# The first MLP of a gated-attention and mixer kernel: preparing the last three weights later in the instruction order

## The chip, the cores and the metric

One core of a Trainium2 chip runs the whole program. The metric is device time in microseconds (us) of one execution. The five engines each take their own instructions in program order: TensorE (PE, with its weight loads as PEld), VectorE (DVE), ScalarE (ACT), GpSimd (POOL) and SyncE (SP), which issues the transfers.

## The reference

A linear attention with decay (its output is x), then a mixer with an MLP (the "first MLP"), then a gated MLP. Cut to what is computed:

```python
for t in range(S):                       # batch 4, heads 8, S 768, D 48
    state = alpha[:, :, t, :, None] * state + np.einsum('bhd,bhe->bhde', k[:, :, t], v[:, :, t])
    y[:, :, t] = np.einsum('bhd,bhde->bhe', q[:, :, t], state)
...
h = x.transpose(0, 2, 1) @ U @ V
u = x + h.transpose(0, 2, 1)             # 768 x 384 for each of 4 batches
x2 = u + np.maximum(u @ w_ch1, 0.0) @ w_ch2      # first MLP: 384 -> 1536 -> 384
...
h = np.maximum(x2 @ w_in, 0.0)
u, v = h[..., :512], h[..., 512:]
v_s = np.einsum('ts,bsd->btd', w_spatial, normalised(v)) + b_spatial[None, :, None]
out = (u * v_s) @ w_out
```

## The kernel before, in words

**Products in three parts.** TensorE multiplies in a short format, so each factor is kept as a high and a low part, and a product is three matmuls (L280 to L282, and L373 for the way up). A weight therefore has to be prepared before use.

**The twelve weights.** The hidden width 1536 of the first MLP is cut into 12 groups; "weight f" is the piece of both matrices for group f, one tile of 128 x 768 words. They arrive as 64-bit numbers. Class `Stage` prepares each in two stages, "begin" and "finish". `begin` issues, in this order, two DVE instructions that build a narrow word (L230 and L233, 128x768), one ACT instruction that scales the low words (L225) and one POOL addition (L240). `finish`, called the first time for a weight, issues an ACT copy, the high part (L586); called the second time, it issues a DVE subtraction, the low part (L245). In the traces and the instruction lists the tile of a prepared weight is `w`; the tenth, eleventh and twelfth weight are `w_1293`, `w_1465` and `w_1644`, and the twelfth is `w_1727` in the changed program.

**The order of the first batch.** The first batch's MLP runs weights 0 to 4 on both halves of the sequence side by side, then the halves in turn: weights 5 to 7, 8 and 9, 10 and 11. For each weight there is a way up (nine matmuls L373 into one of two "mm" banks: three with the high part of the weight and the high part of the input, three with the input's low part, three with the weight's low part), ACT's h (L380), DVE's hl (L361) and, two groups later, a way down (L280 to L282, and L433 when a half is done).

**What is woven in.** Between the matmuls the function `pull` is called. At the call numbers in the table `FIRST_STEPS` it runs `weights.finish` for "f" and `weights.begin` for "b"; from call 71 on it also runs, at an even pace, steps of the attention of the second batch (`attend`). The steps "f" and "b" of one call come ahead of an attention step of the same call. An attention pair (two heads, four pairs for a batch) goes through these steps: transposes (PE L757, ACT L760); the sums per chunk (PE L800, ACT L808), the scan over chunks (DVE L811, six instructions) that follows them, the states (ACT L821, L822); the scores (PE L773) and their masks (DVE L782, two instructions); the outputs (PE L832 with the masks, PE L842 with the states, ACT L857). The decays of the next pair are prepared in between (DVE scans L713 and L726, POOL L702, ACT L732 and L729). The mixer's product of a finished pair is PE L990; it writes the bank that L811 reads its decay factors from. Its low part is DVE L998.

The method that issues a finished weight is short; its two instructions are the two "f" of the table:

```python
def split(w, f=f):
    t = self.parts[f] = self.pool.tile([128, 2, 2 * E], F32R, name="w12", tag=f"f{f}")
    nc.scalar.activation(out=t[:, 0], in_=w, func=AF.Copy)      # L586
    yield
    rest(t[:, 1], w, t[:, 0], nc.vector)                        # L245
```

Of the kernel before, what the change touches and what calls it, by code (L numbers as in the profile page):

```python
# [68 lines left out]
N_WARM = 12  # L69
FIRST_STEPS = {  # L70
    5: "f", 6: "b", 13: "fbf", 22: "fbf", 31: "fbf", 34: "ss", 40: "fbf", 49: "fbf", 51: "ss", 58: "f", 59: "f",
    60: "b", 70: "ff", 80: "b", 89: "ff", 92: "b", 101: "fbf", 110: "ff",
}
AHEAD, N_AHEAD = 71, 4
BANKS = {"acc": 3, "mm": 2, "x": 3}
# [1466 lines left out]
```

## Time and profile before

| | before |
|---|---|
| median of 3 runs | 696.97 us (696.5 to 698.26) |
| profiled execution, its own time | 697.38 us |
| its span, first to last instruction | 695.7 us |
| busy share PE, DVE, ACT, POOL | 98%, 50%, 41%, 28% |
| mean granted clock of TensorE | 0.998 of full speed |

The profiled execution is 0.41 us above the median. A busy share is an average over the whole program; the stretch that the change touches lies between about 100 and 145 us of the span, and there the engines are loaded otherwise.

### The profile page before, as it was taken

To read this page: it belongs to the slowest core of one execution; us is meant where nothing else is said; L and a number is where in the kernel's file an instruction comes from. 1 tells how busy PE (TensorE), PEld (TensorE's weight loads), DVE (VectorE), ACT (ScalarE), POOL (GpSimd) and SP (SyncE) were. 2 spreads that over 40 slices of the span, in tenths; PEclk is the share of its full clock that TensorE was granted. 3 is DMA by queue.
4 is the path that set the end of the run, shared out by engine and by line. 5 is a ranking of instruction groups with operands and counts; after the bars stand their busy time and mean duration, and the time that the engine had idled before them with its cause. 6 is when DMAs were issued, how large, how long until landed. Compare 5 with 4: busy or idle time off the path is not lost.

```text
span 695.7 us, 14559 instructions
## 1 busy us (share of the span) xinstructions
PE 678.7 (98%) x6172; PEld 647.4 (93%) x6172; DVE 351.1 (50%) x651; ACT 283.8 (41%) x554; POOL 195.0 (28%) x165
## 2 busy tenths in 40 slices
PE   8999899999999999999999999999999999999996
PEld 7879898899999999999999999899899989999995
DVE  8989999766456335443333872541343152125211
ACT  3875467665454325554313553322232232123111
POOL 4434334341111131010210332351334223333211
PEclk9999999999999999999999999999999999999999
DMA  8699125333434304101006451401030003000001
GB/s 337 242 337 214 39 50 109 70 70 105 80 58 88 69 1 95 28 2 36 1 0 197 139 168 44 125 1 35 1 102 1 35 0 103 35 1 34 1 35 40
DMA packets 21210, 54.39 MB, mean 78 GB/s; under 512 B 2704, under 2 KB 12816, under 8 KB 19856
## 3 DMA queue, kind: packets, MB, share of 16 engines
q1 hardware_dynamic: 21136, 53.38, 28.3%
q8 instruction: 50, 0.82, 0.5%
q14 instruction: 24, 0.20, 0.1%
HBM read 42.75 MB, written 9.44 MB: 75 GB/s over the span
## 4 chain that ended last, share of the span: by engine, by line
PE 84%; DVE 8%; ACT 3%; DMA 2%; issue 1%; SPq 0%; POOL 0%; ACTq 0%; DVEq 0%
PE banks L373 20%; PE banks L280 18%; PE banks L281 18%; PE banks L282 18%; PE banks L842 2%; DVE bw L713 2%; DMA bits<-in_w 1%; DVE fw L726 1%; PE banks L800 1%; PE banks L832 1%; PE banks L773 1%; PE banks L757 1%; DVE narrow L230 1%; PE banks L974 1%; DVE after L811 1%
## 5 line engine op out<-in xcount | busy, mean ns | idle before, releaser
L373 PE MATMUL banks<-partuh,w 128*128 128x384 f32 x564 | 130.4, 338 | 2.3 <-DVE hl L361 2.3
L373 PEld LDWEIGHTS banks<-partuh,w 128*128 128x128 f32 x564 | 99.4, 188 | 3.7 <-DVE hl L361 2.9
L280 PE MATMUL banks<-h,w 128*128 128x384 f32 x288 | 98.2, 341 | 0.3
L361 DVE SCALAR_TENSOR_TENSOR hl<-banks,h 128x384 fp32r<-128x384 f32 x96 | 52.7, 550 | 86.7 <-ACT h L380 86.1
L281 PE MATMUL banks<-h,w 128*128 128x384 f32 x288 | 96.4, 335 | 0.0
L282 PE MATMUL banks<-hl,w 128*128 128x384 f32 x288 | 96.4, 335 | 0.0
L535 DVE TENSOR_TENSOR vsb<-banks,bb 128x384 f32<-128x384 f32 x32 | 17.9, 558 | 129.1 <-PE banks L282 129.1
L380 ACT ACTIVATE h<-banks 128x384 fp32r<-128x384 f32 x94 | 45.9, 488 | 83.7 <-PE banks L373 83.4
L541 ACT ACTIVATE gh<-gt 128x384 fp32r<-128x384 f32 x32 | 16.8, 525 | 126.2 <-DVE gt L538 126.2
L245 POOL TENSOR_TENSOR gl<-gt,gh 128x384 fp32r<-128x384 f32 x32 | 32.5, 1016 | 120.5 <-ACT gh L541 120.5
L281 PE MATMUL banks<-wsph,vl 128*128 128x384 f32 x192 | 65.1, 339 | 1.0 <-POOL vl L245 1.0
L373 PE MATMUL banks<-partul,w 128*128 128x384 f32 x282 | 66.0, 341 | 0.0
L280 PE MATMUL banks<-wsph,vh 128*128 128x384 f32 x192 | 64.9, 338 | 0.0
L282 PE MATMUL banks<-wspl,vh 128*128 128x384 f32 x192 | 64.8, 338 | 0.0
L245 POOL TENSOR_TENSOR partul<-ub,partuh 128x384 fp32r<-128x384 f32 x43 | 42.9, 1023 | 69.6 <-ACT partuh L316 56.8
L280 PEld LDWEIGHTS banks<-h,w 128*128 128x128 f32 x288 | 54.0, 188 | 1.6 <-issue 0.8
L281 PEld LDWEIGHTS banks<-h,w 128*128 128x128 f32 x288 | 54.1, 188 | 0.0
L282 PEld LDWEIGHTS banks<-hl,w 128*128 128x128 f32 x288 | 54.1, 188 | 0.0
L373 PEld LDWEIGHTS banks<-partul,w 128*128 128x128 f32 x282 | 49.2, 188 | 0.8
L702 POOL TENSOR_TENSOR akq<-akq,fw 128x768 f32<-128x768 f32 x14 | 25.1, 1795 | 77.4 <-DVE fw L726 65.3
L240 POOL TENSOR_TENSOR narrow<-narrow,bits 128x768 uint32<-128x768 uint32 (+1 forms) x14 | 28.4, 2033 | 54.1 <-ACT seen L729 20.5
L245 POOL TENSOR_TENSOR vl<-vt,vh 128x512 fp32r<-128x512 f32 x20 | 27.2, 1386 | 49.8 <-ACT vh L505 49.8
(204 smaller groups left out, 1373.0 us busy)
## 6 DMA issues: line engine op xcount, KB each, us to landing
akq<-in_akq SPq DMA_DIRECT2D x24, 434.4 KB, 7.4
bits<-in_w SPq DMA_DIRECT2D x12, 768.0 KB, 11.6
x2d<-ub SPq DMA_DIRECT2D x8, 576.0 KB, 3.8
ub<-x2d SPq DMA_DIRECT2D x8, 576.0 KB, 4.9
out_y<-ob SPq DMA_DIRECT2D x24, 192.0 KB, 1.9
v<-in_v SPq DMA_DIRECT2D x15, 288.0 KB, 7.6
words<-in_w_in SPq DMA_DIRECT2D x8, 384.0 KB, 3.3
words<-in_wsT SPq DMA_DIRECT2D x4, 576.0 KB, 5.5
```

The lines of the kernel that those rows point to most:

```text
L240: nc.gpsimd.tensor_tensor(out=t, in0=t, in1=low, op=ALU.add)
L245: engine.tensor_tensor(out=out, in0=x, in1=hi.bitcast(F32), op=ALU.subtract)
L280: nc.tensor.matmul(out=ps, lhsT=wh, rhs=xh, start=first, stop=False)
L281: nc.tensor.matmul(out=ps, lhsT=wl, rhs=xh, start=False, stop=False)
L282: nc.tensor.matmul(out=ps, lhsT=wh, rhs=xl, start=False, stop=last)
L361: nc.vector.scalar_tensor_tensor(out=hl, in0=ps[:, 0:TB], scalar=0.0, in1=h.bitcast(F32), op0=ALU.max, op1=ALU.subtract)
L373: nc.tensor.matmul(out=ps[:, 0:TB], lhsT=wx[:, k * 128 : (k + 1) * 128], rhs=ux[:, k, :], start=i == 0, stop=i == len(parts) - 1)
L380: nc.scalar.activation(out=h, in_=ps[:, 0:TB], func=AF.Relu)
L535: nc.vector.tensor_tensor(out=vsb, in0=psv[:, 0:TB], in1=self.g["bb"][:, blk * TB : (blk + 1) * TB], op=ALU.add)
L541: nc.scalar.activation(out=hi, in_=gt, func=AF.Copy)
L702: engine.tensor_tensor(out=chunks(x)[:, c], in0=chunks(x)[:, c], in1=chunks(by)[:, c, 1:CW], op=ALU.mult)
L713: nc.vector.tensor_tensor_scan(out=bw[:, ::-1], data0=a[:, 1 : AW + 1][:, ::-1], data1=ends[:, ::-1], initial=0.0, op0=ALU.mult, op1=ALU.max)
```

## The change

Three steps of the table are put at later call numbers, one at a time: the second "f" of call 89 goes to 93, the "bf" of call 101 goes to 107 (its "f" and "b" in the other order), and the two "f" of call 110 go to 116 and 119.

```diff
 FIRST_STEPS = {
     5: "f", 6: "b", 13: "fbf", 22: "fbf", 31: "fbf", 34: "ss", 40: "fbf", 49: "fbf", 51: "ss", 58: "f", 59: "f",
-    60: "b", 70: "ff", 80: "b", 89: "ff", 92: "b", 101: "fbf", 110: "ff",
+    60: "b", 70: "ff", 80: "b", 89: "f", 92: "b", 93: "f", 101: "f", 107: "fb", 116: "f", 119: "f",
 }
```

No instruction is added or taken away; the transfers' queue (SP) is unchanged. On DVE, at the second attention pair of the second batch, the rows read so (`-` before, `+` changed; `sm` are the masked scores, `narrow` and `bits` the words of a weight that is being begun, here the eleventh):

```order
 L811 SCALAR_TENSOR_TENSOR after<-add,banks 128x96 x6
+L782 TENSOR_TENSOR sm<-banks,causal 128x384 x2
+L230 TENSOR_SCALAR narrow<-bits 128x768
+L233 SCALAR_TENSOR_TENSOR narrow<-bits,narrow 128x768
 L245 TENSOR_TENSOR w_1293<-narrow,w_1293 128x768
-L782 TENSOR_TENSOR sm<-banks,causal 128x384 x2
-L230 TENSOR_SCALAR narrow<-bits 128x768
-L233 SCALAR_TENSOR_TENSOR narrow<-bits,narrow 128x768
 L726 SCALAR_TENSOR_TENSOR fw<-akq_86,starts 128x780
```

The low part of the tenth weight moves from in front of the masks to behind them and behind the begin of the eleventh weight.

On DVE at the third pair, behind the third copy of sums L433 of a finished half:

```order
 L433 TENSOR_TENSOR ub<-banks,ub 128x384 x3
-L230 TENSOR_SCALAR narrow<-bits 128x768
-L233 SCALAR_TENSOR_TENSOR narrow<-bits,narrow 128x768
+L811 SCALAR_TENSOR_TENSOR after<-add,banks 128x96 x6
+L782 TENSOR_TENSOR sm<-banks,causal 128x384 x2
+L361 SCALAR_TENSOR_TENSOR hl<-banks,h 128x384
+L726 SCALAR_TENSOR_TENSOR fw<-akq_84,starts 128x780
 L245 TENSOR_TENSOR w_1465<-narrow,w_1465 128x768
```

The low part of the eleventh weight (L245) moves from in front of the scan L811 to behind the masks and L726, and the begin of the twelfth (L230, L233), which stood ahead of it, comes behind it.

On ACT, from the third pair's outputs to the fourth pair's, the twelfth weight's scaling (L225) and its copy (L586) stand here:

```order
 L729 ACTIVATE seen<-bw 128x12
+L225 ACTIVATE bits<-bits 128x768
 L857 ACTIVATE ub<-banks 48x384 [waits DVE_49,PE_49]
...
 L380 ACTIVATE h<-banks 128x384 [waits PE_49]
-L586 ACTIVATE w_1644<-narrow 128x768 [waits Pool_49]
 L760 ACTIVATE kn<-banks 128x384 [waits DVE_49,PE_49]
...
 L732 ACTIVATE fw,over<-akq_84,below 128x780 [waits Pool_49]
 L380 ACTIVATE h<-banks 128x384 [waits PE_49]
+L586 ACTIVATE w_1727<-narrow 128x768 [waits Pool_49]
 L729 ACTIVATE seen<-bw 128x12
```

The copy L586 moves past the fourth pair's transposes, sums (L808), states (L821, L822), the L732 and the h of the next group. L225 stood before between the two copies L981 ahead of the third pair's L808.

On PE the order is the same; the first three matmuls of the twelfth weight's first way up stand in front of the mixer's product L990 and the fourth pair's outputs, with these waits:

```order
-L373 MATMUL banks<-partuh,w_1644 128x384 x3
+L373 MATMUL banks<-partuh,w_1727 128x384 [waits Activation_49]
+L373 MATMUL banks<-partuh,w_1727 128x384 x2
 L990 MATMUL banks<-yb,u_97 96x128 [waits DVE_49]
 L990 MATMUL banks<-yb,u_97 96x128 x5
 L832 MATMUL banks<-sm,v 48x64 [waits DVE_49] x2
 L832 MATMUL banks<-sm,v 48x64 x22
-L842 MATMUL banks<-akq_84,state 48x64 [waits Activation_49] x2
-L842 MATMUL banks<-akq_84,state 48x64 x20
+L842 MATMUL banks<-akq_84,state 48x64 x22
```

The wait on ACT that stood at L842 now stands at the first matmul with the twelfth weight.

## Rows read from the trace of the kernel before

**Rows 1.** Page, busy us, share of the span and instructions of each engine

```profile
PE 678.7 (98%) x6172; PEld 647.4 (93%) x6172; DVE 351.1 (50%) x651; ACT 283.8 (41%) x554; POOL 195.0 (28%) x165
```

**Rows 2.** Waits of PE, 84 to 150 us: total, times, longest

```profile
PE banks L990 <- DVE after L811: 1.5, 1, 1.5
PE banks L832 <- DVE sm L782: 0.7, 2, 0.5
```

**Rows 3.** Timeline of PE, second pair: start, duration, then the instruction, [idle before]

```profile
109.68 0.31 PE L832 MATMUL banks<-sm,v 64*48 64x64 f32 x2 [0.53 <-DVE sm L782]
110.14 0.90 PE L832 MATMUL banks<-sm,v 64*48 64x64 f32 x46 [0.15 <-DVE sm L782]
110.98 1.46 PE L842 MATMUL banks<-akq,state 128*48 128x64 f32 x44
```

**Rows 4.** Timeline of DVE, second pair

```profile
108.22 0.93 DVE L245 TENSOR_TENSOR w<-narrow,w 128x768 fp32r<-128x768 f32 x1
109.07 1.02 DVE L782 TENSOR_TENSOR sm<-banks,causal 128x384 f32<-128x384 f32 x2
```

**Rows 5.** Timeline of ACT, second pair

```profile
109.53 1.18 ACT L822 ACTIVATE state<-after 64x528 f32<-64x528 f32 x1
```

**Rows 6.** Timeline of DVE, third pair

```profile
118.87 1.60 DVE L230 TENSOR_SCALAR narrow<-bits 128x768 uint32<-128x768 uint32 x1
120.50 0.96 DVE L233 SCALAR_TENSOR_TENSOR narrow<-bits,narrow 128x768 uint32<-128x768 uint32 x1
121.38 0.95 DVE L245 TENSOR_TENSOR w<-narrow,w 128x768 fp32r<-128x768 f32 x1
122.25 1.57 DVE L811 TENSOR_TENSOR_SCAN after<-add,banks 128x96 f32<-128x96 f32 x6
...
127.62 0.56 DVE L361 SCALAR_TENSOR_TENSOR hl<-banks,h 128x384 fp32r<-128x384 f32 x1 [2.89 <-ACT h L380]
128.09 1.77 DVE L726 TENSOR_TENSOR_SCAN fw<-akq,starts 128x780 f32<-128x780 f32 x1
```

**Rows 7.** Timeline of PE, third pair

```profile
123.87 1.55 PE L990 MATMUL banks<-yb,u 128*96 128x128 f32 x12 [1.53 <-DVE after L811]
```

**Rows 8.** Timeline of ACT, third pair

```profile
117.55 0.96 ACT L225 ACTIVATE bits<-bits 128x768 uint32<-128x768 uint32 x1
...
119.10 0.67 ACT L808 ACTIVATE add<-banks 128x576 f32<-128x576 f32 x1
...
127.12 0.47 ACT L380 ACTIVATE h<-banks 128x384 fp32r<-128x384 f32 x1
...
130.35 0.84 ACT L586 ACTIVATE w<-narrow 128x768 fp32r<-128x768 f32 x1
```

**Rows 9.** Timeline of POOL, 118 to 132 us

```profile
118.34 1.72 POOL L702 TENSOR_TENSOR akq<-akq,bw 128x768 f32<-128x768 f32 x1
...
130.01 1.69 POOL L702 TENSOR_TENSOR akq<-akq,fw 128x768 f32<-128x768 f32 x1 [5.99 <-PE banks L373]
```

**Rows 10.** Timeline of DVE, 110 to 137 us, other rows

```profile
110.00 0.55 DVE L230 TENSOR_SCALAR narrow<-bits 128x768 uint32<-128x768 uint32 x1
...
133.02 1.48 DVE L433 TENSOR_TENSOR ub<-banks,ub 128x384 f32<-128x384 f32 x3
134.41 1.77 DVE L713 TENSOR_TENSOR_SCAN bw<-akq,ends 128x780 f32<-128x780 f32 x1
...
136.37 1.52 DVE L811 TENSOR_TENSOR_SCAN after<-add,banks 128x96 f32<-128x96 f32 x6
```

**Rows 11.** Timeline of PE, fourth pair: its sums' end, the twelfth weight's begin

```profile
134.09 0.23 PE L800 MATMUL banks<-ident,nothing 64*64 64x48 f32 x2
...
138.05 0.69 PE L373 MATMUL banks<-partuh,w 128*128 128x384 f32 x3
```

**Rows 12.** Timeline of PE, its last instruction

```profile
688.55 0.34 PE L282 MATMUL banks<-woutl,gh 128*128 128x384 f32 x1
```

**Rows 13.** Windows: stretch, length, busy PE, PEld, DVE, ACT, POOL, granted clock, DMA, GB/s

```profile
692.00:693.00 1.00, 0.00 (x0) 0.00 (x0) 0.00 (x0) 0.00 (x0) 0.00 (x0) 0.73 0.09 27
```

## The prediction

> **What bounds the kernel now.** The page says that TensorE is busy for 98% of the span [rows 1], so the time is PE's own work plus its few idle stretches, and an edit on another engine counts only as far as it moves one of these. The second view is PE's waits in the stretch that the table's late calls touch: two entries stand out there, the mixer's product L990 behind the scan L811 (1.5 us) and the outputs L832 behind the masks (0.7 us) [rows 2]. The third view is the timeline of each engine around the two places, to see what is queued ahead of the instruction that PE waits for. Last, since the change moves one weight's copy a long way down ACT's queue, the timeline at the place where PE first uses that weight. Times below are on the clock of the trace before.
>
> **First move: the masks of the second pair.** DVE does the tenth weight's low part at 108.22 and the masks only at 109.07, 0.85 us later [rows 4]; PE stands 0.53 + 0.15 us for them [rows 3]. With L245 behind the masks these are done 0.85 us earlier and L832 no longer waits. But the next matmuls, L842, need the states, and ACT's L822 ends at 109.53 + 1.18 = 110.71 [rows 5] whatever DVE does behind L811; L842 started at 110.98 [rows 3]. So of 0.68 us at most 110.98 - 110.71 = 0.27 us is gained; the rest becomes a wait on ACT. The bound below is zero. I take **0.25 us**. The moved L245 ends near 111.6 (108.2 + 1.02 for the masks, 0.55 + 0.96 for the begin that is now ahead of it, 0.93 of its own [rows 4, 6, 10]); PE is busy with L842 until 112.4 [rows 3] and reaches the tenth weight only behind it, so that costs nothing.
>
> **Second move: the scan of the third pair.** DVE runs L230, L233 and L245 from 118.87 to 122.25 in front of L811, 3.38 us [rows 6]; L811 then ends at 123.82 and L990 starts at 123.87 after 1.53 us of idle PE [rows 7]. L811's input is ready when ACT's L808 ends, 119.10 + 0.67 = 119.77, or up to 0.8 us earlier, since the L225 of 0.96 us ahead of it is gone too [rows 8]. So L811 starts between 119.0 and 119.8 (I take 119.0; DVE is free at 118.9) and ends by 121.4, before PE arrives at 122.3 - 0.25. The masks behind it (1.0 us) and the two states (2.4 us) end by 122.5 and by 123.8 at the latest, ahead of L832 at about 123.5 and L842 at about 124.3. The whole 1.53 us goes, with about 0.05 more, since a matmul behind a wait does not overlap the one before: **1.55 us**, between 1.2 and 1.6. PE is then 1.8 us ahead.
>
> **Third move: the twelfth weight.** Here a wait is added. PE meets this weight at 138.05 [rows 11], with the gains at 138.05 - 1.8 = 136.25. Before, ACT copied it (L586) at 130.35 [rows 8], long ahead. Now the copy stands behind L821, L822, L732 and L380 of the fourth pair, and L821 waits for that pair's L811. How long this takes is read from the third pair: from L811's start (122.25) to L380's start (127.12) 4.87 us, then 0.47 for L380 and 0.84 for L586 [rows 6, 8]: the weight is ready 6.2 us after the fourth pair's L811 starts. Queued behind the waiting matmul on PE are L990 and the outputs L832 and L842, all of which could have run; nothing else is late for them.
>
> When does that L811 start? From the third pair's (119.0), along DVE's new order, start to start:
> - to L361: 5.37 (122.25 to 127.62, ACT's chain) = 124.4; L361 0.47 and L726 1.77 [rows 6] = 126.6; L245 0.95 = 127.55.
> - L230. POOL's L702 becomes ready 1.92 us behind L726's start (128.09 to 130.01) [rows 6, 9], here at 126.8, while L245 runs. Alone L230 takes 0.55 us [rows 10]; at 118.87, begun during an L702 that ran from 118.34 to 120.06, it took 1.60 and ended 0.41 behind it [rows 6, 9]. If L702 runs as soon as L245 ends, to 129.2, L230 ends at 129.65; if L230 goes first, at 128.1.
> - L233 0.96; then L998 and L361, about 0.7 together; L433 to L713 1.39, L713 to L811 1.96 [rows 10]: 129.65 + 0.9 + 0.7 + 1.4 + 1.95 = **134.6**, less some 0.1 of overlaps, 134.5.
>
> In the other case DVE is ready 1.5 us earlier, and what L811 then waits for is its input, at 133.2 (the bound below). So PE gets its weight at 134.5 + 6.2 = 140.7, less 0.1 for the overlap of L380 and L586: 140.6. It stands from about 136.3 to 140.6, **4.3 us**, and the program is 140.6 - 138.05 = **2.5 us** behind before from there on.
>
> On L230 the Trainium skill (SBUF — State Buffer, "Who interferes with whom") says that the port pair that VectorE and GpSimd share is an exclusive lock: the one that starts first has it for its whole instruction and the other is blocked. The 1.60 us of L230 agree. By that rule the sum is 2.5; with shared bandwidth and no lock it would lie between 1.4 and 2.5.
>
> **The sum.** 4.3 - 1.8 = 2.5 us longer. Own time of the profiled execution 697.38 (span 695.7 and 1.68 around it), so 699.9 for it; it was 0.41 above the median of 696.97, and on the median the forecast is **699.5 us**. Bounds without another mechanism: the fourth pair's sums on PE end at 134.32 [rows 11], with the gain at 132.5; L808 (0.7) follows, so L811 starts at 133.2 at the earliest, and with 6.1 us behind it the weight cannot come before 139.3, 1.3 us late. At the other end L811 may start at 134.9 and the second move give only 1.2: 3 us. What remains of the program is bound by PE, so that nothing gives this back: the other engines only gain room. The twelfth weight's low part is used some 4 us behind its high part (L990, L832 and L842 stand between: 1.55 + 0.9 + 1.46 [rows 3, 7]) and DVE needs 0.95 for it: nothing.
>
> **The rivals.**
> - *A shorter wait.* L230 goes ahead of POOL, or DVE's rows overlap more; L811 starts at 133.2, the weight comes at 139.4, and the loss is 1.35 us: **698.3**. For it: DVE's next instruction is already in its queue. Against: in the trace POOL had the port whenever it came first, and here it has waited since 126.8.
> - *The clock falls in the wait.* PE's last matmul ends at 688.89 [rows 12]; in 692 to 693 the granted clock averages 0.73, a fall from full (2.4 GHz) to half (1.2 GHz) at 692.46, 3.6 us behind it [rows 13]. The mean of the whole span is 0.998 of full speed, so the wait of 1.53 us did not lower it noticeably. A wait of 4.3 us could, and the matmuls behind it would take twice as long until it rises. No row shows how long that lasts; from below nothing, and I take a low clock of 3.6 us, as long as the idle before the fall, a choice: 1.8 us more, **701.3**. The Trainium skill (TensorE: Matmul & The Clock Gate, "Why this matters for your kernels") warns of long idle gaps between bursts of matmuls, which speaks for this rival.
> - *The copy is in time.* Only the gains are left, 697.0 - 1.8 = **695.2**, faster. That needs L586 done by 136.25, so the fourth pair's L811 begun at 130.1, before PE has even made the sums that it scans (132.5). It would take a chain of 3.3 us instead of 6.2 from L811 to the copy and no DVE work ahead, so I hold it for nearly excluded.
>
> **How the numbers follow.** The forecast 0.58, with a range of its own of 698.8 to 700.2; the shorter wait 0.18; the fallen clock 0.20; the copy in time 0.04. A difference of 0.3%, 2.1 us, is about what a measurement of this kernel tells from none; the bound lies at 699.1, inside the forecast's own range, so some eight of ten of its chance count as slower (0.48), with the fallen clock's 0.20 in all 0.68. The rest of the forecast and the shorter wait make 0.28 for the same, and 0.04 remain for faster. The range of 698.1 to 701.4 takes in the three cases that are slower in some degree.
>
> **What the profile of the changed kernel would show.** Right: no idle of PE before the third pair's L990, at L832 of the second pair at most a trace, a short wait of L842 on L822; one idle stretch of 3.8 to 4.6 us before the L373 that stands ahead of the fourth pair's L990, put down to ACT's L586; that L586 directly behind an L380; the fourth pair's L811 at about 134.5; L230 of the twelfth weight at 1.6 us or more, ending with POOL's L702. Clock: 1.00 from 130 to 150, or a window under 1.00 near the end of the wait. Wrong it would be if the copy's wait is under 2 us, if L990 still waits for L811, or if a second wait of PE appears in the fourth pair's outputs or the mixer's sums behind.

## The result, and the profile after

The changed kernel takes 704.62 us (median of 5 runs, 702.6 to 706.71), the kernel before 697.28 (5 runs, 696.5 to 698.26): a ratio of 1.0105, 95% interval 1.0091 to 1.012, so 7.3 us slower where 2.5 were forecast. The profiled execution is the longest of the five: 706.71 us, with a span of 704.9 against 695.7. Its accounts below must come to 9.2 us, not to 7.3.

PE's waits from 84 to 180 us of the changed kernel (total, times, longest):

```profile
PE banks L373 <- ACT w L586: 3.0, 1, 3.0
PE banks L757 <- issue: 2.4, 1, 2.4
PE banks L832 <- issue: 0.5, 1, 0.5
PE banks L990 <- ACT yb L981: 0.3, 1, 0.3
```

Of [rows 2] the wait of L990 behind L811 is gone, as forecast, and the forecast wait for the twelfth weight's copy L586 is there, with 3.0 us for 4.3. A second wait of 2.4 us, at L757 (the fourth pair's transposes), was not forecast. Its releaser is given as "issue", so the view names no cause. PE's timeline has the places:

```profile
110.43 0.96 PE L832 MATMUL banks<-sm,v 64*48 64x64 f32 x37
111.94 0.42 PE L832 MATMUL banks<-sm,v 64*48 64x64 f32 x11 [0.55 <-issue]
112.29 1.45 PE L842 MATMUL banks<-akq,state 128*48 128x64 f32 x44
...
123.53 1.47 PE L990 MATMUL banks<-yb,u 128*96 128x128 f32 x12
...
132.45 0.85 PE L757 MATMUL banks<-ident,akq 128*128 128x128 f32 x6 [2.44 <-issue]
...
135.12 1.16 PE L373 MATMUL banks<-partuh,w 128*128 128x384 f32 x3
...
137.83 0.79 PE L373 MATMUL banks<-partul,w 128*128 128x384 f32 x3
...
144.79 1.33 PE L373 MATMUL banks<-partuh,w 128*128 128x384 f32 x3 [3.01 <-ACT w L586]
145.92 2.76 PE L990 MATMUL banks<-yb,u 128*96 128x128 f32 x12
```

Besides the two waits, look at the durations. L990 took 1.47 us at 123.53 and 2.76 at 145.92 for the same twelve matmuls, and three L373 took 1.16 and 1.33 where the undisturbed ones take 0.69 [rows 11]. Windows of one microsecond say why (stretch, length, busy PE, PEld, DVE, ACT, POOL, granted clock, DMA, GB/s):

```profile
84.00:85.00 1.00, 1.00 (x5) 1.00 (x4) 1.00 (x3) 0.00 (x0) 0.00 (x0) 0.50 0.00 0
135.00:136.00 1.00, 1.00 (x5) 0.98 (x4) 0.64 (x2) 0.00 (x0) 0.00 (x0) 0.50 0.02 8
137.00:138.00 1.00, 1.00 (x49) 0.95 (x50) 0.84 (x2) 0.73 (x3) 0.26 (x1) 0.91 0.00 0
144.00:145.00 1.00, 0.21 (x1) 0.21 (x2) 0.79 (x2) 0.85 (x3) 0.00 (x0) 0.51 0.00 0
...
150.00:151.00 1.00, 1.00 (x28) 0.93 (x22) 0.00 (x0) 0.00 (x0) 0.00 (x0) 0.58 0.06 16
```

The granted clock is at half (1.2 GHz) behind each wait: from 133.8 to 137.2 behind the wait at L757, and from 144.0 to 150.8, beginning within the wait for L586. A third stretch, 82.6 to 86.0, lies before the place of the change, behind a wait of 2.3 us (L373 behind L361) that the profile of before has too, there with the clock at 1.00.

On DVE and ACT the timeline shows what the two waits hang on. DVE first:

```profile
120.60 1.58 DVE L811 TENSOR_TENSOR_SCAN after<-add,banks 128x96 f32<-128x96 f32 x6 [0.31 <-ACT add L808]
...
128.16 0.93 DVE L245 TENSOR_TENSOR w<-narrow,w 128x768 fp32r<-128x768 f32 x1
129.01 2.04 DVE L230 TENSOR_SCALAR narrow<-bits 128x768 uint32<-128x768 uint32 x1
131.08 0.96 DVE L233 SCALAR_TENSOR_TENSOR narrow<-bits,narrow 128x768 uint32<-128x768 uint32 x1
132.07 0.28 DVE L998 TENSOR_TENSOR stk<-banks,stk 32x128 fp32r<-32x128 f32 x1
...
138.69 1.57 DVE L811 TENSOR_TENSOR_SCAN after<-add,banks 128x96 f32<-128x96 f32 x6 [0.82 <-ACT add L808]
```

Then ACT, and POOL:

```profile
137.97 0.69 ACT L808 ACTIVATE add<-banks 128x576 f32<-128x576 f32 x1 [0.24 <-PE banks L800]
...
143.91 0.83 ACT L586 ACTIVATE w<-narrow 128x768 fp32r<-128x768 f32 x1
...
128.38 2.24 POOL L702 TENSOR_TENSOR akq<-akq,fw 128x768 f32<-128x768 f32 x1 [7.03 <-DVE fw L726]
```

L998 takes the mixer's product of the third pair out of its bank, and it now stands behind L245, L230 and L233. It ends at 132.07 + 0.28 = 132.35, and L757 starts at 132.45. The code says that the two share a bank: the product's bank is `ps_g` in place `ALONE`, and `tags = {"flip": (ALONE, PAIR[0])}` gives that place to the transposes of the next pair. Before, L998 ended at 130.28 and L757 started at 130.38, the same 0.1 us behind it, and PE had no idle there. The rows of the kernel before, of DVE and of PE, which the account below uses too:

```profile
130.00 0.28 DVE L998 TENSOR_TENSOR stk<-banks,stk 32x128 fp32r<-32x128 f32 x1
```

```profile
106.43 0.93 PE L773 MATMUL banks<-akq 64*64 64x64 f32 x48
...
130.38 0.85 PE L757 MATMUL banks<-ident,akq 128*128 128x128 f32 x6
...
134.25 0.80 PE L373 MATMUL banks<-partul,w 128*128 128x384 f32 x3
```

**The account.** Differences of the same instruction's start, after minus before, along PE, in the two profiled executions: scores L773 of the second pair +1.35 (107.78 against 106.43: the low clock at 82.6 to 86.0); L842 +1.31; L990 of the third pair -0.34; L757 of the fourth +2.07; the L373 five microseconds behind it +3.58 (137.83 against 134.25); the twelfth weight's first L373 +6.74; the next L373 with that weight +9.61 (151.79 against 142.18); the span +9.2. So the first move brought 0.04, the second 1.65; the wait at L757 cost 2.4 and the low clock behind it 1.5; the wait for the copy cost 3.2 and the low clock behind it 2.9. The two waits less the two gains are 3.9 us and the low clock behind the waits is 4.4; the 1.35 us of the stretch at 82.6 lie ahead of the change, and 0.4 us are gone again by the end.

### The profile page after: what moved, and what is told of

Its sections match the earlier page's. It is cut to its first block, busy times and chain, and to the rows that moved or that the text cites. A ratio compares the mean times of both kernels' runs of the same rounds, so it can differ in the third digit from the quotient of the medians.

```text
span 704.9 us, 14559 instructions
## 1 busy us (share of the span) xinstructions
PE 685.3 (97%) x6172; PEld 653.4 (93%) x6172; DVE 351.8 (50%) x651; ACT 283.8 (40%) x554; POOL 194.7 (28%) x165
## 4 chain that ended last, share of the span: by engine, by line
PE 86%; DVE 5%; ACT 3%; DMA 2%; issue 1%; POOL 1%; SPq 1%; ACTq 0%; DVEq 0%; POOLq 0%
PE banks L373 20%; PE banks L280 18%; PE banks L281 18%; PE banks L282 18%; PE banks L842 2%; PE banks L800 1%; PE banks L832 1%; PE banks L773 1%; PE banks L757 1%; DVE fw L726 1%; DMA bits<-in_w 1%; DVE bw L713 1%; PE banks L974 1%; PE banks L393 1%; PE banks L990 1%
## 5 line engine op out<-in xcount | busy, mean ns | idle before, releaser
L373 PE MATMUL banks<-partuh,w 128*128 128x384 f32 x564 | 132.3, 343 | 5.3 <-ACT w L586 3.0
L373 PEld LDWEIGHTS banks<-partuh,w 128*128 128x128 f32 x564 | 100.7, 190 | 7.0 <-ACT w L586 3.3
L361 DVE SCALAR_TENSOR_TENSOR hl<-banks,h 128x384 fp32r<-128x384 f32 x96 | 52.6, 549 | 86.5 <-ACT h L380 85.9
L380 ACT ACTIVATE h<-banks 128x384 fp32r<-128x384 f32 x94 | 45.8, 488 | 85.4 <-PE banks L373 85.1
L373 PE MATMUL banks<-partul,w 128*128 128x384 f32 x282 | 66.5, 343 | 0.0
L245 POOL TENSOR_TENSOR gl<-gt,gh 128x384 fp32r<-128x384 f32 x32 | 32.4, 1014 | 120.6 <-ACT gh L541 120.6
L245 POOL TENSOR_TENSOR partul<-ub,partuh 128x384 fp32r<-128x384 f32 x43 | 42.8, 1022 | 75.7 <-ACT partuh L316 63.0
L373 PEld LDWEIGHTS banks<-partul,w 128*128 128x128 f32 x282 | 49.6, 189 | 0.8
L702 POOL TENSOR_TENSOR akq<-akq,fw 128x768 f32<-128x768 f32 x14 | 25.6, 1827 | 80.6 <-DVE fw L726 80.6
L245 POOL TENSOR_TENSOR vl<-vt,vh 128x512 fp32r<-128x512 f32 x20 | 27.1, 1381 | 49.8 <-ACT vh L505 49.8
```

What stands on the lines that cost most here:

```text
L245: engine.tensor_tensor(out=out, in0=x, in1=hi.bitcast(F32), op=ALU.subtract)
L361: nc.vector.scalar_tensor_tensor(out=hl, in0=ps[:, 0:TB], scalar=0.0, in1=h.bitcast(F32), op0=ALU.max, op1=ALU.subtract)
L373: nc.tensor.matmul(out=ps[:, 0:TB], lhsT=wx[:, k * 128 : (k + 1) * 128], rhs=ux[:, k, :], start=i == 0, stop=i == len(parts) - 1)
L380: nc.scalar.activation(out=h, in_=ps[:, 0:TB], func=AF.Relu)
L702: engine.tensor_tensor(out=chunks(x)[:, c], in0=chunks(x)[:, c], in1=chunks(by)[:, c, 1:CW], op=ALU.mult)
```

## The experiments

Each was compared with the kernel before on its own chip (medians 698.31 of 14 and 698.34 of 23 runs there), so the ratios are what to compare, not the times.

**The begin one call later.** Theory: L757 waits for L998, which stands behind the twelfth weight's begin. The rival was a wait for POOL's L702 or for the port that DVE and POOL share; a reason of PE's own, as the word "issue" would have it, would leave the wait as it is too. At call 108 the two steps come behind L998.

```diff
-... 101: "f", 107: "fb", 116: "f", 119: "f",
+... 101: "f", 108: "fb", 116: "f", 119: "f",
```

> The changed kernel with one step moved by one call, 107 to 108, so that the mixer's low part L998 stands on DVE ahead of L245, L230 and L233. Theory: the 2.44 us of idle PE before the fourth pair's L757 are a wait for L998, which reads the bank that L757 writes. Then that wait is gone (under 0.3 us), the wait for the twelfth weight's copy L586 grows from 3.0 to about 4.2 us, since PE comes to it earlier, and a clock fallen behind one wait costs about 3 us: 702.8 us, 701 to 704. Rival: L757 waits for POOL's L702 (the q of the same pair) or for the shared port. Then moving L998 alone does nothing, the wait stays at 2.0 to 2.8 us and the time near 704.6.

Measured: 703.67 us, ratio 1.0074 (1.0057 to 1.009). PE's waits, then DVE's timeline, then PE's:

```profile
PE banks L373 <- ACT w L586: 4.5, 1, 4.5
...
```

```profile
129.63 0.28 DVE L998 TENSOR_TENSOR stk<-banks,stk 32x128 fp32r<-32x128 f32 x1 [1.30 <-ACT stk L997]
129.95 1.04 DVE L245 TENSOR_TENSOR w<-narrow,w 128x768 fp32r<-128x768 f32 x1
```

```profile
130.02 0.85 PE L757 MATMUL banks<-ident,akq 128*128 128x128 f32 x6
...
142.31 1.33 PE L373 MATMUL banks<-partuh,w 128*128 128x384 f32 x3 [4.48 <-ACT w L586]
143.43 2.76 PE L990 MATMUL banks<-yb,u 128*96 128x128 f32 x12
```

With L998 ahead of L245 the wait at L757 is gone: it was L998. The rival, POOL's L702, is out, since here it ended at 130.18, behind the start of L757 at 130.02. The wait for the copy is now 4.5 us, close to the forecast's 4.3, since PE comes to it 2.4 us earlier. The clock fell in it, at 140.4, with PE idle since 137.8, and stayed at half to 147.2; L990 again took 2.76. From the first L373 to the next behind L842 it is 148.82 - 142.31 = 6.5 us, before 4.13 (142.18 - 138.05): 2.4 us for the clock.

**The copy at call 112.** The other wait by itself: the wait at L757 stays, and the copy L586 comes early enough.

```diff
-... 107: "fb", 116: "f", 119: "f",
+... 107: "fb", 112: "f", 119: "f",
```

> The changed kernel with the twelfth weight's copy L586 at call 112 in place of 116, so that ACT runs it between the two copies L981 of the third pair and ahead of the fourth pair's states. Theory: the wait of 3.0 us before the first matmul with the twelfth weight is gone, and with it the clock that fell behind it; the wait before L757 stays at 2.4 us, with a clock fall of up to 1.5 us behind it. Sum against before: 2.4 - 1.65 = 0.75 without and 2.3 with the fall: 698 to 699.6 us. Rival: the loss comes from the port shared by DVE and POOL and not from the copy's place; then at most 1 us is given back, 703.6 or more.

Measured: 699.6 us, ratio 1.0017 (1.0004 to 1.0031). PE's waits:

```profile
PE banks L757 <- issue: 2.4, 1, 2.4
...
```

The wait of 2.4 us stays, the one for L586 is gone, and the clock is at half from 133.4 to 136.8. Less the second move's 1.65 us, the wait makes 0.75 us and the clock about 1.5, 2.2 in all; 1.2 were measured (0.3 to 2.2). The ten executions suggest why it is less. Their mean granted clock is 0.993 in the profiled one and up to 0.998 in others, and the two with 0.998 have spans of 695.6 and 696.4, which is what the kernel before takes on that chip at a mean clock of 0.997 or 0.998 (694.9 to 695.7) plus about 0.75. So the wait of 2.4 us seems to have lowered the clock in some executions only; no trace of those is kept.

**Only the copy late.** The kernel before with the third move alone.

```diff
-... 101: "fbf", 110: "ff",
+... 101: "fbf", 116: "f", 119: "f",
```

> The kernel before with only the last two steps of the change: the two finishing steps of the twelfth weight at calls 116 and 119 in place of 110. Nothing is gained ahead. Theory: the fourth pair's L811 starts at 136.4 us of the span as before, the copy is ready 6.1 us later, and PE stands 4.3 us before its first matmul with the twelfth weight: 701.6 us without the clock, and about 704 (702.5 to 705) with a clock fallen at the end of that wait for some 5 us. No other wait of PE is added. Rival (the clock falls by chance wherever it falls, in before too): 701.6 us with the mean granted clock at 0.998.

Measured: 702.18 us, ratio 1.0055 (1.0032 to 1.0078). PE's waits:

```profile
PE banks L373 <- ACT w L586: 3.0, 1, 3.0
...
```

Then ACT's and DVE's timelines:

```profile
136.00 0.69 ACT L808 ACTIVATE add<-banks 128x576 f32<-128x576 f32 x1
```

```profile
136.72 1.58 DVE L811 TENSOR_TENSOR_SCAN after<-add,banks 128x96 f32<-128x96 f32 x6
```

The time lies below the expected 702.5 to 705, because the wait was 3.0, not 4.3: with the begin at its old place and the low part at 119, DVE was free when the fourth pair's sums came, and L811 started 0.72 us behind the start of L808. So 3.0 us is the wait with an undelayed L811. In the run at call 108 L811 started at 136.31, 1.6 us behind the end of L808, and DVE was busy up to it: the other 1.5 us of that run's wait stem from the eleventh weight's low part and the twelfth's begin, which stand in front of it there. The clock, 144.2 to 147.6 at half, makes the rest: 702.18 - 698.31 is 3.9 us. Here too one of the five executions has a mean clock of 0.998, and its span of 698.4 is that of the kernel before at such a clock plus the 3.0 us of the wait alone.

**Filling the waits with matmuls.** Is the low clock caused by the idle of PE? Matmuls whose results nobody uses were put in both waits of the changed kernel. If the idle is the cause, the waits remain in the time and the low clock goes.

```diff
+                if isinstance(b, int) and b == 0 and blk == 0 and f == NF1 - 1:
+                    busy(6, ps.banks[:, 3, :])
                 h = self.up_group(block, f)
...
+                if n == 2 * NP - 1:
+                    busy(5, ps.banks[:, 3, :])
                 pair.flip()
```

> The changed kernel with extra matmuls that need nothing and whose result is not used (identity by identity, about 0.44 us each at full clock): 5 ahead of the fourth pair's L757 and 6 ahead of the first matmul with the twelfth weight, so that PE has work in both waits. The waits themselves stay. Theory: the falls of the clock follow from the two idle stretches; with PE busy in them the granted clock stays at 1.00 from 125 to 155 us, and the time is before's plus 2.4 + 3.0 - 1.65 = 3.8, near 701 us (700.3 to 702.3). Rival: the falls come from elsewhere (the load of PE ahead, or the phase of the run); then the clock falls there as often and the time stays within 1 us of 704.6.

Measured: 704.69 us, ratio 1.0086 (1.0069 to 1.0103): a miss. PE's waits (the lines from the first insertion on have moved by two; L740 are the added matmuls):

```profile
PE banks L740 <- DVE hl L363: 2.9, 1, 2.9
PE banks L759 <- issue: 1.4, 1, 1.4
```

The second group waited itself, 2.9 us, for a bank that `hl` still read, and lengthened the path by its own time; the clock fell to half behind it (145.1 to 148.5). The first group filled 1.28 us of the first wait (0.26 us for each matmul, not the expected 0.44) and left 1.4 idle, and there the clock stayed at 1.00. So the run says something of the first wait and nothing of the second. With larger groups and a free bank for the second:

```diff
-                    busy(6, ps.banks[:, 3, :])
+                    busy(11, ps.banks[:, 4, :])
...
-                    busy(5, ps.banks[:, 3, :])
+                    busy(9, ps.banks[:, 3, :])
```

> The changed kernel with extra matmuls in both waits, as in the filled kernel before but with the second group in the bank that is free by then, and with counts for 0.26 us each as measured there: 9 ahead of the fourth pair's L757 and 11 ahead of the first matmul with the twelfth weight. The results of the extra matmuls are not used. Theory: the clock falls follow from idle PE; both waits stay as time (2.4 and 3.0 us), the granted clock stays at 1.00 from 125 to 160 us, and the time is that of before plus 3.2 to 3.8 us: about 701.5 (700.3 to 702.3), some 3 us below the changed kernel. Rival: the falls are not due to idle PE; the clock falls in 125 to 160 us all the same and the time stays at 704 or more.

Measured: 701.77 us, ratio 1.005 (1.0031 to 1.0069). PE's timeline, and windows:

```profile
130.22 2.17 PE L740 MATMUL banks<-ident 128*128 128x128 f32 x18
132.85 0.85 PE L759 MATMUL banks<-ident,akq 128*128 128x128 f32 x6 [0.46 <-issue]
...
140.49 2.62 PE L740 MATMUL banks<-ident 128*128 128x128 f32 x22
143.69 0.79 PE L375 MATMUL banks<-partuh,w 128*128 128x384 f32 x3 [0.58 <-ACT w L588]
```

```profile
135.00:136.00 1.00, 1.00 (x16) 0.80 (x17) 1.00 (x3) 0.05 (x1) 0.00 (x0) 1.00 0.09 31
144.00:145.00 1.00, 1.00 (x10) 0.99 (x9) 1.00 (x2) 0.00 (x0) 0.00 (x0) 1.00 0.07 16
```

L759 starts at 132.85 (132.45 in the changed kernel), since what it waits for is no earlier; the twelfth weight's L375 starts at 143.69 (144.79), since the matmuls between ran at full clock. The clock is at 1.00 from 87 to 170, and three L375 behind the wait take 0.79 and not 1.33. All four executions have a mean clock of 0.995 to 0.998, as those of the kernel before have; the five of the changed kernel have 0.990 to 0.996. The time falls from a ratio of 1.0105 to 1.005. So the waits, less the gains, cost 0.005 x 698 = 3.5 us, and the low clock behind them the other 0.0055 x 698 = 3.8 us (with the two intervals roughly 1.5 to 6). The waits are as long with the fillers and the clock stays up, so the idle of PE is what lowers it.

**The first move alone.**

```diff
-... 89: "ff", 92: "b", 101: "fbf", 110: "ff",
+... 89: "f", 92: "b", 93: "f", 101: "fbf", 110: "ff",
```

> The kernel before with only the first step of the change, the tenth weight's low part at call 93 in place of the second step of call 89. Theory: PE's wait for the masks (0.68 us) goes and is replaced by a wait of 0.45 to 0.9 us inside L832, behind its 37th record, as in the traces of the changed kernel, so that L842 starts no earlier relative to the scores: same as before within 0.3 us. Rival (the prediction's own account: L842 bound by the states): L842 starts 0.25 us earlier and the time is 0.25 us less.

Measured: 698.49 us, ratio 0.9999 (0.9987 to 1.0011). PE's timeline:

```profile
110.70 1.52 PE L832 MATMUL banks<-sm,v 64*48 64x64 f32 x48
112.14 1.69 PE L842 MATMUL banks<-akq,state 128*48 128x64 f32 x44
...
125.47 1.55 PE L990 MATMUL banks<-yb,u 128*96 128x128 f32 x12 [1.74 <-DVE after L811]
```

From the start of L773 (108.05) to the end of L842 (113.83) it is 5.78 us, before 6.01 (106.43 to 112.44): 0.23 gained, as forecast. But L990 then waits 1.74 and not 1.53 us [rows 7], so 0.21 are handed back there, where L811 still sets the time. The time is the same, as this run's theory said, but not by the wait inside L832 that it named: the view shows none there. The rival had the earlier L842 right and the time wrong.

**A better table.** If both costs come from DVE and ACT work standing in front of something that PE needs, the twelfth weight's begin belongs ahead of the third pair's L361, where DVE was idle for 2.89 us [rows 6], the low part of the eleventh behind L998, and the copy before the fourth pair's chain.

```diff
-... 101: "f", 107: "fb", 116: "f", 119: "f",
+... 101: "f", 105: "b", 108: "f", 110: "f", 119: "f",
```

> The kernel before with the steps so placed that neither of the two new waits should arise: the tenth weight's low part behind the second pair's masks (call 93), the twelfth weight's begin right behind the third pair's masks, where DVE is idle (105), the eleventh's low part behind L998 (108), the twelfth's copy at 110 as before and its low part at 119. Theory: the 1.5 us before the third pair's L990 are gained and nothing is lost: 1.6 us under before, and no clock fall from 100 to 160 us. Rival: any weight work moved behind the third pair's masks delays the fourth pair's chain; then a wait of 1 us or more shows before L757 or the twelfth weight and the time is no better than before.

Measured: 696.36 us, ratio 0.9977 (0.9966 to 0.9987): by the ratio 1.6 us faster than before, and so faster than both kernels. DVE's timeline, then PE's:

```profile
122.43 0.55 DVE L230 TENSOR_SCALAR narrow<-bits 128x768 uint32<-128x768 uint32 x1
...
128.05 0.28 DVE L998 TENSOR_TENSOR stk<-banks,stk 32x128 fp32r<-32x128 f32 x1 [1.28 <-ACT stk L997]
128.36 0.96 DVE L245 TENSOR_TENSOR w<-narrow,w 128x768 fp32r<-128x768 f32 x1
```

```profile
122.01 1.47 PE L990 MATMUL banks<-yb,u 128*96 128x128 f32 x12
...
128.43 0.84 PE L757 MATMUL banks<-ident,akq 128*128 128x128 f32 x6
```

L990, L757 and the twelfth weight's L373 have no wait, the second move's gain stays, L230 takes 0.55 us in DVE's gap, and in the profiled execution the clock does not fall from 70 to 170.

## Why the prediction was wrong

**What failed.** Two steps. The larger is the clock: the sum put its term at nothing, and the rival "the clock falls in the wait", whose mechanism was right, got the lesser chance (0.20). Its ground was that "the wait of 1.53 us did not lower it noticeably", which says nothing of longer waits. The rival was also sized too small: 1.8 us for a wait of 4.3, where the run at call 108, with that wait alone, shows 2.4. Without anything else this gives 1.0074, 5.2 us, against the 2.5 forecast. The other step is in the third move: it asked what stands behind the copy on PE ("nothing else is late for them"), but not who waits for L998, which it counted only as time on DVE ("L998 and L361, about 0.7 together"). L998 releases the bank that L757 writes. That added a wait of 2.4 us and a second fall of the clock. The sign was right for a reason that held, the wait for the copy; but the sum had one of the four costs, and the rival two.

**First move.** Forecast 0.25, in the profile 0.04. The masks came early, as said, and alone the move gave 0.23 at L842 (first-move run), lost again in the wait of L990. In the changed kernel PE pauses 0.55 us within L832, behind the 37th of its matmul records, with "issue" as releaser; that is not a wait on ACT's L822. The same place shows in the traces of all other runs but the one with the first move alone, with 0.3 to 0.9 us, the run with only the copy late included (0.3), whose order at this pair is the old one; so it does not hang on the change, though the trace of before has none. In the run with the first move alone the 48 L832 took 1.52 us where the third pair's took 0.89, so a part of it may be there too. What it is stays open.

**Second move.** Forecast 1.55, measured 1.65. L811 started at 120.60 in place of 122.25, and L990 without a wait.

**Third move, the copy.** The mechanism was right: L586 follows an L380 behind the fourth pair's states, and PE stands for it ahead of L990. The size of 4.3 us is near what it is without the wait at L757 (4.5, call 108). In the changed kernel it is 3.0, because the first wait holds up PE, and the chain from L800 to L586, which the bound of the sum named, sets the rest: L811 waits 0.82 us for L808 and starts at 138.69, not at 134.5 (some 1.35 us of this are the low clock at 82.6).

**L230 and POOL.** Forecast: L230 runs against L702 and ends 0.41 behind it. It took 2.04 us and ended 0.43 behind L702 (131.05 against 130.62); in the better table it took 0.55 with no POOL work beside it. The Trainium skill (SBUF — State Buffer, "Who interferes with whom") calls the port pair that the two engines share an exclusive lock, and these rows agree with that. The step was sound, but the 1.5 us that it put on DVE were a part of what reached PE through L998.

**The warning on idle gaps.** The Trainium skill (TensorE: Matmul & The Clock Gate, "Why this matters for your kernels") warns of idle gaps between bursts of matmuls. The granted clock agrees in every trace in which a wait of 2.4 us or more at these two places was left unfilled. The gaps that the page warns of are longer than the 2.4 us behind which the clock fell here, so by the measurement shorter ones can do it too.

## What to carry to other kernels

When work is moved on an engine that runs in order, list every instruction that comes to stand behind it, and for each one who waits for it, the next writer of the bank that it reads included; a wait that the profile calls "issue" can hide such a reader. Count an idle stretch of TensorE of a few us twice, as its own length and as the low clock that may follow it: in the traces here 1.5 to 2.9 us behind waits of 2.4 to 4.5 us, though by their mean clock not in every execution. Put movable work where its engine stands idle for another one, as the 2.89 us in front of L361, and not merely behind the instruction that it was in the way of.

## What the hardware showed unasked

- The clock can fall after PE has resumed: L757 started at 132.45 and the fall came at 133.8, 1.4 us later; it lasted 3.4 us. Behind the wait of 3.0 us in the same execution it lasted 6.8 us, as behind the one of 4.5, but 3.4 behind the 3.0 us of the run with only the copy late.
- The same wait does not always lower it. The wait of 2.3 us at 80 us left the clock at 1.00 in the profiles of before and of the better table, but at half from about 83 to 86 or 87 in the other seven. It lies ahead of the stretch that the prediction looked at (84 to 150 us); there it would have spoken for a clock that holds. Of 23 executions of the kernel before, 13 have a mean clock of 0.995 or 0.996 and spans of 696.6 to 697.4, the other ten 0.997 or 0.998 and 695.0 to 695.7; where the clock fell in those no trace shows. A part of the scatter between executions of one kernel is of this kind.
